# Fused sliding-window attention and cosine-gated MLP on one core: masks of four units written by ScalarE, x of eight units by DMA, and a new order of work

## The chip, the cores and the metric

The kernel runs on one core of a Trainium2 chip. The metric is the device time of one execution in microseconds (us); a comparison takes the median of several runs. The engines are named as in the profile: PE (TensorE, matmuls), DVE (VectorE), ACT (ScalarE), POOL (GpSimd) and SP (SyncE, which here only issues DMAs).

## The reference

Eight batches of eight heads, 576 tokens, 64 columns each. Attention has a window of 128 tokens and a bias that falls linearly with the distance; its output, as x (4608 tokens by 512), goes through an MLP with a cosine gate.

```python
scores = scale * np.matmul(q, k.transpose(0, 1, 3, 2))
bias = slopes[:, None, None] * (-np.abs(rel).astype(np.float32))[None, :, :]
mask = (rel >= 0) & (rel < window)
scores = np.where(mask, scores + bias[None], -1000000000.0)
attn = np.exp(scores - np.max(scores, axis=-1, keepdims=True))
attn = attn / (np.sum(attn, axis=-1, keepdims=True) + 1e-09)
x = np.matmul(attn, v)          # to (4608, 512)
h = x @ w_in                    # (512, 2048)
out = (h * np.cos(h)) @ w_out   # (2048, 512)
```

## The kernel before

**Attention** is cut into units. A batch has nine: four pairs of heads times G = 0 or 1 (the first and the second 256 tokens), and a tail of 64 tokens. A unit's score (L529 for a tail, L539) goes to two PSUM banks; ACT takes the exponential (`exps`, L590, L598); DVE multiplies by a mask table `emask` that holds window and bias together (`mask`, L611, L623; the table is built at the start, L460 and L465); PE multiplies by v (`pv`, L640 to L656); DVE divides (`norm`, L681 to L712). Two units share one score op, which waits as a whole for all that it reads. x is then transposed for the MLP, by PE with a copy on ACT or DVE (`x_pe`, L742 to L753) or by a DMA transpose on SP (`x_dma`, L762, L768). There is an older second way for the mask: `seed` (L554 to L579) has ACT write the scaled distances `dif` into the banks, the score adds to them, and the unit has no multiplication. The setting `SEEDN` says for how many pairs of units of a phase the first unit is seeded; it is empty here.

**q, k and v.** Batches 0 and 1 are transposed on PE (`qk_transposes`, L483, copies L500/L501). From batch 2 on, q and k are loaded as they lie (`load_nat`, L385, five DMAs each for `qnat` and `knat`) and transposed by two DMAs on SP (`dma_transposes`, L396 and L399, to `qt` and `kt`). v is loaded in five tiles (`load_v`, L375). All loads are issued by POOL, all DMA transposes and stores (L1095) by SP. Buffers are double, so batch b reuses those of batch b - 2.

**The MLP** runs over nine chunks of 512 tokens. The first product is L975 (chunk 0), L782, or L876 in a form with fewer products from chunk 6 on; ACT takes the cosine (L787, L940, L980) and DVE multiplies (L791, L943, L984). The second product is L1067 (L1161 for chunk 0), with sums made by DVE (L1003, L1031, L1046), a copy or sum (L1052, L1090) and the store.

**Order.** Attention of batch 0 comes first; then phase c (0 to 5) of attention, with 8, 10, 10, 12, 14 and 9 units, goes with chunk c. This program order only says what each op reads and writes. What runs when is said by a text at the head of the file, `TABLE`: `follow` decodes it into one list of all ops, and for copies that either ACT or DVE may do, into the engine. `emit` puts each engine's ops into its queue in this order, with waits on semaphores where another engine's op or a DMA must be done. Every queue is in order: an op that waits holds up everything behind it on its engine, and on POOL and SP this includes the DMAs behind it.

The settings that the change touches are read in `attention`:

```python
if g // 2 < SEEDN.get(phase, 0):
    two = sorted(two, key=lambda u: u[1] == "t")
    seed(two[0], 0)
...
first = (S * u[0] + (512 if u[1] == "t" else 256 * u[2])) // CH
after.append((first > phase + 1 or g < XD.get(phase, 0), u, ub, n))
```

Here `g` counts the units of a phase in steps of two, S is 576 and CH 512; a unit whose entry is true goes to `x_dma`.

Of the kernel before, what the change touches and what calls it, by code (L numbers as in the profile page):

```python
# [14 lines left out]
B, H, S, D = 8, 8, 576, 64  # L15
# [12 lines left out]


TABLE = (  # L30
    'c-nPV2Y6If7JmPfH!Wo*A%PHdEHqifjs=k}tV#(GFqBXPBn4$bu`FK_%_4*%1ObV(K#D*JSt&-E!h-'
    '0xDvPKfD@{Z`QYO7kX6D^JciMYzU|;fHUhcd1+;jf_Kj&N_3_w#jJy552L+3%Pc;zlP#H-yktj(-'
    'pEjqM{ck}PJwCrB3q-'
    '{9M;&d$5qHR9WADS}~;_2H1xbO#`q+wdtgon`B>6%HyG|f?3%VnDsdnr<5N0St5ZZ)?8zmXNGD<Zg2=y6N`U+Gy?'
    '$F$*GyJWJoN!r+3anTS_iMU&FrmJy)q1{k##U*rYHRJHq^Dy35b!Y@oPU}o$A?_9;n<O%5Xs0l2&{m^^1BgNm_9P'
    '~pqObs4C1TN&{Qy{6(86~%nA#%H5NW^O=4`d2vLnc~h(_}2&mQcz_^`@$G{b79x#rnLjt-93Hcj0-'
    'yv%|m2e+*e0cZK}!+72b)WUaJT8@pXD+fk0N6bOV1gB(Si4?NA5T2-'
    '!JB(zEKr!Mj%{>;HUNYjab!Z7$qCql;L3G!CjefR+FFk(bw73vr<2ntCbb8MB)_5dQYyf6J%<J=0tY;ul(MgN&rc'
    'O0s&EiG$uIcm#Y~Vab;v#yqnaVrE7GY>V-A}Btqa`;P_Nv&jvF#{*7WM`>VMkre&#)Wy?uO_aV#gax-'
    'm{4=v5trFP6j>R?Tw2c0rY#J*M(j<PaOY>o)>#w^hUa2)xJ2kX>J~-'  # L40
    '#3SczLYEI#)13`0UMgZCvSU&r@KXVhQx8AYHOt^~S#t385v1pL)39f1&X4(!RY_VSn%~;N7Le~0Vt5k)3C!7qncH'
    'Sb_KKyP6<WQBL=(H{om`}^2hwehkBNkN1f6-'
    '=6Jf`#n1*9F&|{#~8ip5b`?XFO3>mnmKg4fqM&X#D2BXTu`vb#MxEL-'
    '2=FZh<=U!>)?uhVjo~ev?pC0h90j^d!W2#$W>Vg}3Lez;yMB~`dF58D5!*GHZ4bkokcrZJo8XMBIs3+J`c0!*&!='
    'cNak2M(+9t6%k<c;_TI5&xT-;_~SjMe)zLQ?kr-'
    '9G)}so_oZgT~!nS)>B%(>F{i(nL<%Kma6dPT_kIY8xqVGm@6sSZY)QY;}3kyZHF!JjrNbPWohF6A1kpQae^Jz>4Y'
    'nMq|4ag_#Z%abX$X0Qx{bdg5-'
    'w!C^Sy0wzSSv6YO*7!5g5KOZPW>L)jeqDWi^PVfHiNt_&bV&I7<#pb?el1f*R3lvbBscPqQM6(|M=#E!7MQtWiEo'
    '^$q8jetWg{{laSk`ID;w6<lHL!It@CI3ZRWxET-dy=6bdfZi^BN)-'
    'kx6rkxYh^Af7Y$CX%W0qP@nf!;+_cuy#JAV$$(>L5)aS8M@n1a32RRL3Yb{W0a`!VJ8|o4{JEnxs(L});p(&v8a9'  # L50
    'u_yO{KZHL$YuW?tu(Sy-'
    '!vCGTmAdZpg4wXLtycpkG<<E5@OtDZg=!_1h1+Njmjw*z0aL)7QnhFOPv(elHPlI>oe%EXgvk}suL+RHI+l!oPEe'
    'ttc)y)KY7q-'
    'GO9HpEp~!82*s>_!_J5TR{@5f%EL7h^Wh(4l4fbO%j~jd783&`#My06C4>3;+Is6L%3tT|^hYe#$tr1&iB&6{dwW'
    'wmj!;Baz_4=p8Jja_9ps>tY{=<;GUvOwSAXGq+K`;>!KNrH|ImXY(ASTzHFN^apdvpSj*r6^VK)$8H@P=`NPcPO&'
    'XkYSBhFw`irt0gqb!LQPqlVQC7VwU?z)4yP6n<)+6xUk=rH29r)HJ=#nkkufV0J5o_@v9wsQWd0@&P$WT0e*0vOC'
    'WIl=#9la*x}LDtWaQG=0xl2(#f%Kz3QWi+K|tR$xwKh#_K~ywPUk>V_~X988-'
    'dL$7M*|kTUzrMQ~>ttJm@GYT>9QFLiQ#JGHIu^Q5UX9joXGsV+1N~s5tf4rg&Z0t843@yK)VUZ;eO{vvf>bj#_<{'
    'E{YJE13lG{)N}UY3D6Y>lsCkRX4ja{$9_e$IQETy;j`zD56VwIGwJ{vRRhIkkY72;<?OL;WxyDsbjLJ`d?#gik4L'
    '%OwvOj>3X-Yk5pe`ia}jeHouYwjx-lYe?zUO*6w~{=z!E<7?VOdoJcyIBk3;YN22T&Udsl*?z2EoT*eN`VQ(2lOw'  # L60
    '$ie!%Cd#CND}y^H-5G~apWoVM#%(x$>q1=4UeA7@v$>FHVpXpRNz-`z1w9-2S&rNI|0<^yIkuIxJ1&2qr-'
    'yn-P&*BAkwbEg<YgZWM`B<Ux7!?;yxT0hEB9Poq9_H<xB+6$<+&1*V*jXQ=!i##UhbBC-HxJ9b4f>O5FQM$GVlYY'
    '0;EzOMeT$+Oi@ir?~G>em;QF`Fb7Uw0-'
    ')DSUv5QX5E;wvHsQX@ok50m+CO*%wR0XM0gH$JNq(o?|pd}rcrfU%@Ny^NS$EwY}9WNlRrb}CwAb0!CyUIkX8zeE'
    't`lBMNi5`Z9289jS-byN0#8`Z0-K46!6u51NJvfI*I<pVOKD}#Bep<(EjKAJ>#OvyA?}aT-'
    'Eb<QtZWG>gAiq@nZu|-Z>5YIIxXgTPJ-Qv8(%8OF{x~utj?J<T~4~q=Mu!G!`B%o{U^X7EYfMjy|cFw5l`KlR}P!'
    'Ka8_mW<8uzKs|eA|5Ic*_e7cdlcU3q+K^v!GU5I4-4igxj^A<ASLge=;<iQSZL!w7=WR?W#-'
    'vXhCLeN@7x(>g+{qRDABl6lLS<Fw>!h`LQKaFe(HMu)ipAva=P&;AW;|7_8}?>Xa&1&CWqRI3oTyJm0VHkMj~b-'
    'KU~R;VLVn(IO$x|2XD-#Cwa~YvoxGM@0FUnOnlZXB(9|3jhMQu{ARUV7(DVnyPJ@o)_f&pP-'
    '0v1&I@q5tK0fHEZqW2B6vpePz;Nsr3p!)OwvLraMQ%IB0%b!Fk8kvD!^ICX(d5SU`>)JBl;A)3x!^A~*gA1H!Njk'  # L70
    '9bb31AJ#9jLnSFn5nJP8V+>6WI*{{9$K=-'
    'Ii4(}ekB>9rlTbz8;dAV@$vsGY#Mm*p3)v9cI)0mEeyn;9Sk1Ej+_{IEB=6m(OWM%qp|L4FkV=POcUwRSz4?%tjO'
    '!EE7%nJVFo1y$1xLEKDW3+%V*`a_(LEi!<eA{Ja22J?)4@RI|7PRIIN8a6UkTIrQNx^0MmIX}Gdse33v8*ibI3(}'
    'Q6!`hQq7VFL0TWDyL%1z)LEb|Fqa2QJsRyz<9M$)jGC(Gyq6mu#GUiIyWiMn}lrw_vC^2CnX65Kq(JOA5auqsW#('
    'az6gPr;3Fs3vS*iFTO!lleCE-fW~K`s@;f-'
    'DuL7*vWwMFvwo)YDYK%Ys!&lL=}a$qa_Dqe_$j$%4|P%7Sk&C^p7|E-05OoaEoQU{w(_HKhuIl)N)0L6E?If-ndQ'
    'f>bOkomPRMj6=zXYB;2Fs8S$=8>KAS9bxj%$jo92RQykW$_h$ynL-'
    ';1n|B~0C{NjJ5M;#~HD{_qDyS92ASr8Q=(}$hf?wlN8Dh7U35CEE3Rb4eZHcVrLB=YO&ys+EVM&F9-'
    '>_E|awkyN8>TE$>Y^ZLfm%hXRv?#4)t*Y5EYzr4%5w1xWK3uw7gWYn<tfyI;9|8HRZ>;#t145fwkp%W<gb}oO8Vt'
    ';%~TDI391Zd3iT@kVuEmcuME+!AOkCeh?Xh408{MGRAGcvK=>2_;SOCz;Xi5FXBMh@##BcNK~)Hu608vNLvl*BDH'  # L80
    'GHNRFy;B3gs%n{7pj$fl+x7VWHhmHY6$LK<1t&5`BViq8BRfR0)!TR`@J<FZkbrVSDq@w=+*W79u-'
    'AsdYv9Vyey(st|R(RU84Bg0wsI(4aO|@>6G)${!)5eW-e@5K<&=Z_fWO<s>k5KMFa_g&GrXJ7L|{Z-'
    'kIjkN?mA0G*W>_y'
)


# [166 lines left out]
def bass_alibi_sliding__then__act_gcu_kernel(  # L253
# [8 lines left out]
    with ExitStack() as ctx:  # L262
        def sb(name, shape, dt=BF16):
            return ctx.enter_context(nc.sbuf_tensor(name, shape, dt))

        R = Plan(nc, ctx)
# [5 lines left out]
        FAST, SPRI, GS = range(1, NCH), 3, 4  # L272
        FAST1, WPRI, KPRI, APRI, MPRI, GPRI, TPRI, LPRI = range(6, NCH), 4, 1, 2, 4, 4, 4, 5
        KENG, DPEN, CENG = ("act",), 0, ("act", "dve")
        JN, PRE2, SEEDN, XD, LORD = (5,), (), {}, {4: 6}, 0
        SDPRI, NH, LWPRI, G1, S4IN, SPLIT = 1, 2, 2, 1, True, True
        TRIPLES = [(2, 3, 4), (5, 6, 7)]
        WGS = 4
# [8 lines left out]
        xT = sb("xT", [128, NPAIR, XR], F16)  # L287
# [16 lines left out]
        P = [Pall[:, i, :, :] for i in range(NP)]  # L304
# [938 lines left out]
        for c in range(NCH):  # L1243
# [26 lines left out]
            n = QUOTA[c] if c < len(QUOTA) else 0  # L1270
# [54 lines left out]
```

## Time and profile before

| what | us |
|---|---|
| runs | 299.79, 300.42, 299.76 (median 299.79) |
| the profiled execution | 299.71 |
| its span, first to last instruction | 298.0 |
| PE busy | 287.9 (97%) |
| DVE busy | 262.1 (88%) |
| ACT busy | 222.1 (75%) |
| POOL busy (issue of loads included) | 95.2 (32%) |

Line numbers are those of the kernel before; after the change the same lines have a number higher by one, as the new table is a line longer. In a row of the timeline the columns are start, duration, engine, line, operation, output <- input, shape and count, and in brackets the idle time of the engine before it and what ended it. In a row of the groups they are busy time and mean nanoseconds of one, then the idle time before. In a row of the DMA issues the last number is the median time from issue to landing. Busy times by stage have a start and end, the length, and then busy time and instructions of each engine in turn.

### The profile page before, as it was taken

The numbers are of one execution on the slowest core, as the hardware profiler recorded it, in microseconds if no ns is written. First come the engines' busy times: TensorE is split into PE (matmuls) and PEld (weight loads), VectorE is DVE, ScalarE is ACT, GpSimd is POOL, SyncE is SP. The second block draws the span as 40 slices with busy tenths as digits, with TensorE's granted clock in tenths as the row PEclk, the third lists the DMA queues.
The fourth block names the chain that finished last, engine by engine and source line by source line (L and its number), as shares of the span: only waits on it lengthen the run. The fifth ranks groups of instructions, "written<-read, shape, count | busy, mean of one in ns | idle before, by whom it ended". The sixth has DMA issues, their size and how long they took to land.

```text
span 298.0 us, 7278 instructions
## 1 busy us (share of the span) xinstructions
PE 287.9 (97%) x2974; PEld 205.2 (69%) x2974; DVE 262.1 (88%) x522; ACT 222.1 (75%) x318; POOL 95.2 (32%) x122
## 2 busy tenths in 40 slices
PE   2899999999999999999999999999999999999996
PEld 2678845446874586458854788547768888888884
DVE  3879877599977999899999999999999999999972
ACT  5788878689757889688777878579778758778620
POOL 7997000599642303991195005000000000000000
PEclk9999999999999999999999999999999999999999
DMA  7999999999999994999999939973131400041033
GB/s 153 173 205 208 207 169 146 180 196 155 136 175 147 130 187 90 142 173 173 169 170 133 163 85 130 159 164 74 21 79 21 150 2 0 2 141 37 10 134 106
DMA packets 147729, 37.96 MB, mean 127 GB/s; under 512 B 133360, under 2 KB 146416, under 8 KB 147696
## 3 DMA queue, kind: packets, MB, share of 16 engines
q0 software_dynamic: 99344, 18.10, 79.7%
q1 hardware_dynamic: 48352, 19.41, 34.5%
q8 instruction: 23, 0.38, 0.5%
q14 instruction: 10, 0.08, 0.1%
HBM read 36.70 MB, written 9.44 MB: 155 GB/s over the span
## 4 chain that ended last, share of the span: by engine, by line
PE 94%; DVE 2%; POOL 1%; issue 1%; ACT 1%; POOLq 0%; DVEq 0%
PE ps L1067 33%; PE ps L782 24%; PE ps L876 11%; PE ps L539 5%; PE ps L975 5%; PE ps L1161 4%; PE ps L653 3%; PE ps L656 2%; PE ps L742 2%; PE ps L483 2%; PE ps L529 1%; DVE kt L501 1%; PE ps L640 1%; PE ps L642 1%; PE ps L1138 1%
## 5 line engine op out<-in xcount | busy, mean ns | idle before, releaser
L1067 PE MATMUL ps<-w_outb,gT 128*128 128x256 f16 x512 | 82.3, 273 | 0.0
L782 PE MATMUL ps<-xT,w_inb 128*128 128x512 f16 x336 | 82.2, 379 | 0.0
L787 ACT ACTIVATE cos<-ps,halfpi 128x512 f32<-128x512 f32 x84 | 54.9, 687 | 18.9 <-PE ps L782 13.9
L598 ACT ACTIVATE p<-ps 128x768 bf16<-128x768 f32 (+1 forms) x64 | 55.6, 915 | 11.5 <-PE ps L539 9.5
L791 DVE TENSOR_TENSOR gT<-ps,cos 128x512 f16<-128x512 f32 x84 | 54.5, 686 | 5.5 <-ACT cos L787 5.1
L1067 PEld LDWEIGHTS ps<-w_outb,gT 128*128 128x128 f16 x512 | 48.2, 98 | 12.5 <-issue 1.3
L782 PEld LDWEIGHTS ps<-xT,w_inb 128*128 128x128 f16 x336 | 31.7, 98 | 31.1 <-DVE gT L791 1.5
L375 POOL DMA_DIRECT2D vp<-in_v_dram x40 | 34.3, 892 | 53.1 <-PE ps L656 35.3
L1067 PE MATMUL ps<-wsum,gsum 128*128 128x256 f16 x256 | 38.5, 273 | 0.0
L623 DVE TENSOR_TENSOR p<-p,emask 128x768 bf16<-128x768 bf16 (+1 forms) x64 | 38.0, 615 | 0.3
L385 POOL DMA_DIRECT2D qnat<-in_q_dram x30 | 25.5, 918 | 23.9 <-DMA qt<-qnat 23.9
L1052 ACT ACTIVATE ob<-ps 128x512 f32<-128x512 f32 x33 | 19.6, 598 | 13.7 <-PE ps L1067 11.2
L385 POOL DMA_DIRECT2D knat<-in_k_dram x30 | 25.7, 948 | 9.3 <-DMA kt<-knat 7.0
L1067 PEld LDWEIGHTS ps<-wsum,gsum 128*128 128x128 f16 x256 | 23.2, 98 | 4.0 <-issue 0.5
L876 PE MATMUL ps<-xT,w_inb 128*128 128x256 f16 x132 | 24.8, 273 | 0.0
L696 DVE TENSOR_TENSOR xnats<-ps,rec 128x256 f16<-128x256 f32 x56 | 21.9, 420 | 0.5
L539 PE MATMUL ps<-qt,kt 64*128 64x128 bf16 (+1 forms) x320 | 20.1, 253 | 1.3 <-DVE kt L501 1.3
L653 PEld LDWEIGHTS ps<-vp,p 128*128 128x128 bf16 x256 | 16.0, 99 | 4.3 <-issue 1.0
L653 PE MATMUL ps<-vp,p 128*128 128x65 bf16 x256 | 18.9, 196 | 0.1
L1067 PE MATMUL ps<-wsum,gT 128*128 128x256 f16 x112 | 18.1, 273 | 0.0
L539 PEld LDWEIGHTS ps<-qt,kt 64*128 64x128 bf16 x320 | 11.9, 98 | 8.6 <-issue 3.6
L1161 PE MATMUL ps<-w_outb,gT 128*128 128x512 f16 x64 | 17.6, 380 | 0.0
(111 smaller groups left out, 478.0 us busy)
## 6 DMA issues: line engine op xcount, KB each, us to landing
out_dram<-ob SPq DMA_DIRECT2D x35, 256.0 KB, 2.7
vp<-in_v_dram POOLq DMA_DIRECT2D x32, 128.0 KB, 6.9
qnat<-in_q_dram POOLq DMA_DIRECT2D x24, 128.0 KB, 7.1
knat<-in_k_dram POOLq DMA_DIRECT2D x24, 128.0 KB, 10.8
w_inb<-in_moe_w_in_dram POOLq DMA_DIRECT2D x4, 512.0 KB, 10.5
w_outb<-in_moe_w_out_dram POOLq DMA_DIRECT2D x4, 512.0 KB, 21.8
gsum<-in_q_dram POOLq DMA_DIRECT2D x1, 576.0 KB, 15.5
gsum<-in_k_dram POOLq DMA_DIRECT2D x1, 576.0 KB, 17.6
```

Of the source, the lines that this page charges most:

```text
L375: op("pool", [lambda e, t=t, rows=rows: e.dma_start(vp[b % 2][0:rows, t, :, 0:64], v[b, :, 128 * t:128 * t + rows, :].rearrange("h p d -> ...
L385: fns.append(lambda e, t=t, rows=rows: e.dma_start(nat[which][b % 2][0:rows, t, :, :], src[b, :, 128 * t:128 * t + rows, :].rearrange("h p ...
L539: ins = e.matmul(ps[:, banks[x], c0:c1], keys_ap(b, x, pr, kc), query_ap(b, x, pr, qb, 128 * nb), start=c0 == 0 and (b, pr, G) not in seed ...
L598: op("act", lambda e: e.activation(P[i][:, :, 0:hi], src_[:, :, 0:hi], ACTF.Exp, scale=0.125), w=held + [("P", i)], occ=920 if G else 691, ...
L623: op("dve", lambda e: e.tensor_tensor(p, p, m, ALU.mult), r=[("EM", h0), ("EM", h1)] + ([] if G else [("EM2", h1)]), w=[("P", i)], occ=600 ...
L653: ins = e.matmul(o, P[i][:, x, d0:d0 + 128], V[:, kc, h, 0:65], start=True, stop=not two)
L782: op("pe", lambda e, kc=kc: e.matmul(ps[:, bank, :], w_in[:, kc, 128 * fc:128 * fc + 128], xT[:, kc, r0:r0 + CH], start=(kc == 0), stop=(k ...
L787: op("act", lambda e: e.activation(cosb[ci][:, :], ps[:, bank, :], ACTF.Sin, bias=halfpi[:, 0:1]), r=["halfpi"], w=[("B", bank), ("cos", c ...
L791: op("dve", lambda e: e.tensor_tensor(gT[gi][:, fc, :], ps[:, bank, :], cosb[ci][:, :], ALU.mult), r=[("cos", ci)], w=[("B", bank), ("g", ...
L876: op("pe", lambda e, i=i, kc=kc: e.matmul(ps[:, bank, 256 * i:256 * i + 256], left(kc, p0 + i), right(kc), start=(start and i == 0 and kc ...
L1067: op("pe", lambda e, t=t, p=p: e.matmul(ps[:, bank, 256 * t:256 * t + 256], left(p, slice(128 * t, 128 * t + 128)), right(p), start=(start ...
L1161: op("pe", lambda e, t=t, fc=fc, bank=bank: e.matmul(ps[:, bank, :], gT[gi][:, fc, 128 * t:128 * t + 128], w_out[:, fc, :], start=(fc == 0 ...
```

## The change

Two settings and the order. `SEEDN` becomes `{3: 2, 4: 2}`: the first unit of each of the first two pairs of phases 3 and 4 is seeded. In phase 3 these have G = 0 (two activations of 256 and two of 128 columns each), in phase 4 G = 1 (two of 512 columns each), twelve activations in all; their four multiplications at L623 go. `XD` becomes `{4: 6, 5: 2}`. The table is written anew for the list of ops that results.

```diff
 TABLE = (
-    'c-nPV2Y6If7JmPfH!Wo*A%PHdEHqifjs=k}tV#(GFqBXPBn4$bu`FK_%_4*%1ObV(K#D*JSt&-E!h-'
...
+    'c-nnd30PF+8b0qVXP9BwA-'
...
-        JN, PRE2, SEEDN, XD, LORD = (5,), (), {}, {4: 6}, 0
+        JN, PRE2, SEEDN, XD, LORD = (5,), (), {3: 2, 4: 2}, {4: 6, 5: 2}, 0
```

What the new table holds, decoded: the same 2974 matmuls in another order; three copies of q and k transposes and three copies of x more on ACT and fewer on DVE, and one copy at L1052 fewer on ACT and one more on DVE; 36 DMA transposes of x, as before. On POOL the load of v tile 3 of batch 6 stands ahead of the five loads of K of batch 6, where it stood behind them; on SP K's transposes of batch 6 stand behind seven transposes of x and one store after Q's, where they stood behind three transposes.

More of the change, by code (lines that the diff above doesn't have):

```diff
@@ L30 @@
 TABLE = (
-    'c-nPV2Y6If7JmPfH!Wo*A%PHdEHqifjs=k}tV#(GFqBXPBn4$bu`FK_%_4*%1ObV(K#D*JSt&-E!h-'
[L32 to L80, printed above, removed]
@@ L81 @@
-    'GHNRFy;B3gs%n{7pj$fl+x7VWHhmHY6$LK<1t&5`BViq8BRfR0)!TR`@J<FZkbrVSDq@w=+*W79u-'
-    'AsdYv9Vyey(st|R(RU84Bg0wsI(4aO|@>6G)${!)5eW-e@5K<&=Z_fWO<s>k5KMFa_g&GrXJ7L|{Z-'
-    'kIjkN?mA0G*W>_y'
+    'c-nnd30PF+8b0qVXP9BwA-'
+    '4>*)GWQJZJOO~H?=I(a4EegAf{rX;T1(KyNr4>Ma^)<Oi>FE(nQIn$GWy?i{@@O(=^lESY{YtU}j*>f4~3CFmuk}'
+    'a}Uf}{{4Hu_kI6gFdLd-H^bE|vSuLeR(p-nqer8uQPkCS#ntL?kErc{%66X0-'
+    '^{H21D>m$wO8UQI)C%`It{*h<{oJ3!x|*5WHzBTq8MloeqD<PG)x23qW@J*L~KQu)0!|%r}|hE;K1bvOh5OeR(0V'
+    'gsbhB_<cB^d9y7r8ljc#nhrpS+^pcha?G*ye<zBo?XhUejMQVAWHx6kAX{qz=c68Imeu~QHacFo|8zWycj7~(<8e'
@@ new lines @@
+    'nkSsyZSLwW87a+`$(QzIfDW<jsMaDA=Oqw;n&PoE>jNRE-Ojco?>}ZbLY$zZGpqg!RpLwO#6}cqCD9#^M@`<98zE'
+    'Q%9r8%*NVyc{oZn>;;6^(R(OR57!q%%M<A1%Rx*NQp#6Pi)RU-'
+    'c|V2+QNv2dpblXuk)RRb)<h1fJ&Yb_r4ZiK$h0i7FKFrm5)$l@`)7!2sP~l6vpCG=U}gIE=l*v16}}vOH3b)KyU|'
+    '$`_1N|t^k#=SOb+b^qTGhf$sCrt=4d!PKnzeF+gLs@w4poJrPLsDa`%g~J6dC`d2gaD1C?g*3_%|bSLW)hZb^7+8'
+    'Ma~ix(hw<i=4-'
+    '<{B{8k{)$}Kvo#Id@xevp1L;~Uo!_kIwNB$1w@1?~Mpy5ne4E)bZiCL_?za)?rni<*)?k{CnAtz~oV}9roqJoi9Q'
+    'O4Y5x}ff$Zj*?Na9LV4Be}h+9KrvSYuF)7%PQYgW1v+JF=wsJL@?tw92`JlYVvmymi2WnsxShG4CLgFfuuh9>XJN'
@@ new lines @@
+    '>Ae6w#HXC!nyu!)YT-'
+    '#dKcM{S6TcT^;E1~(!)c{uy0H4+=t+pt%EOz)N<;T^#5Z(=v%^iqLQfQ~g~5)Fm9Epna6N|VTzL2z(6PcD7vjQM#'
+    'EZsSamSQRW3gjI84~y4I#R`Hd2MVN#d<9M*Wyg~-'
+    'h+SPu$)34V5)oiqbGN;k$c!!8BU1c^v3pAO!<lBl8L#cP&UfcX!6!>n6`F&u{6C9NX~y9gi#IXzJ%gluq-'
+    '`lNwfn^QVbhYFblQ<QdcUcVcnLQt1~ySq4_mW+B6d)us)+EY6}{uIs|8!J8XdKM03CIa9V5{jV}h5nFmiEocwW=v'
+    'l+S(Z7PA)$Xs1`3|mn9>od3`uj2fudYEBzApShDUmvBjMc0CIJ)*G0D&;QC)H+coMu<z7Rfupn%+`)bJJa)|;Zg<'
+    'A4oyVuISXi%H8XRfZLq+y&_b9lCmieUp+K}V<vBvU0cWg#8=;!)^P2Zo&fmoQ`Y(GV@NMxs3!s6h$(@@@nv1lTq}'
@@ new lines @@
+    '#dhVBZPX$Q{}lw+=jC7L!ziU8Ci!avjpOjfL7sV<D{aeXF&wfBQoiy$P?&RgF7S2-uAwL`r8m*-'
+    'R;i5Nl`f`Dn(CtP!EiXp82qFr7cR<VNlhDX85EW4)-'
+    'Fj`sUTGqCCFXS9#}DB%;g*&#Z_a@*%y*Zq_5(|LN4a@xk7L{IS?qQoXb3ht62R0A}{If-'
+    'M{&_&W$a~$bWPkA_pUc@3j#~PD1!|`&_y*Ij{E;jMst1=9$fSImEOWwlUM88F}Qc?z8Vf7$PjmYpZXWFc#D+#d+5'
+    '6w-(gFXoV1Uh)%X06I%4O)qU&Z<Iebu8#k#TEF(l?*h*ZNV50uZ-;qkiQs0C)Dg^6YSABYv$M0+-'
+    'HEKoz4e3e)w6PgvVs4*P_~pIrXb%(Ys?MB46WDZ_JBHwiZf8w`82#$kXgJlJSx)qj3e#xsxamHPL9|buN&HtSWV5'
+    '{65E+Mhy!s)_Gh%<r;`2J>ES9^d2#z&$S1CwV*g@`{ajyxpUjz;m*b^^F0lvxpT!kBvnvIn)bJVyqS?$o~=jrhTS'
@@ new lines @@
+    '9eoJN(WpTM!+w3{_LkX2Lx1N6k{LW~DK0#eH<wJ9G(@rYiGs1Mtb+>E>|ph~|fZEKoCJUB3Mf7F2Q^jv;Jho{B%O'
+    '~M5IP~O@sQ<J;Vt~4^v@VapB=ym(h_tcr*ecObU0WSkPlD%Y$bC_2Xmfe3(gWPaKa#+1QL~Su^3UP@BAd!Xu@?Wp'
+    'n?Ses+mq(rFFP*;>^Ont9wvIsBlRE`J^ryc~AbM<m>g|{CL-xBEQ0d*zcx>orT9Iw2GR3j}sU+B%53`$a1cN(8+O'
+    'Kv7t`N}Be;zS~KhJWFHS4>Eo+&3wJUpa{K095Hzvg^;_S`G?FPryAm&@ehZS~s7IV<ce&$5vGA@ed$_vwA63#2^S'
+    'I~Q6OT9H=`in;Hp9GQ&UQ*-XW0(9nTF>n7q#@g*tw@F**W3ou&>$Xi;dvj6K?RlG)S;-'
+    'Tzc%kRDZ8?7+e$j+&)36@RZ{$<Nf40*-'
@@ new lines @@
+    'dZ`<Jnrr>=u@mNL%g4Z@^XwX1l1dxWOk4E(AmgY)A;!hLCnlk29JZ$xClxnme2`8=Sfi(%u6D`=Nk>P7{Q6GSuGs'
+    '1~*2IKfpFv3|jTllorWCL4`u<)Ww;aTXBMgPc^SwrT)v+CkC>v2aCUif2oVnQD^TrXPr^7r9<+ju!&}7Nj`*O4Xv'
+    'tcNh2<PQF&wraVnmoI4L^AO>>BkEw+AVwg^xs}Wg!qqLs}Bu-Vb4?webVMhJ}p*Kix1Ouxl?1T>)#xT*oT0h@x<|'
+    'pHjm>taBC30z{G-'
+    'qS$OHdivJ9prrCp6KjQirmv^w_v;U4fl8HR*Pe>6pp2<Z+tjXk8#Cgi(!VZxf^Nr*2aXL2AF(wm5T={LQ$cmA&_+'
+    'Nw<>PmFDiHC=mV-'
+    '&FSl}6&&WaMk{NKb8<13e$7eKTz<rjkmxrp;PaGWO^dba}R5{En0Zw>vv4#~#0Of9;UZZ;FUL_hi@TokX6mx@OUN'
@@ new lines @@
+    '?8`x44myU~L0><MLu4h~Ne^5@3ckXPi3Jm##kkKoa4XWOcpnn>Cve_5N%Z>@4ES`EcQYh%6r~XUDactw-'
+    '&?M{<0#>*X4-LbgT0_dbDvUOM)@d5SNyRg>(>#!EtN8MQQM8le#p-'
+    'yF232i4ZexIJ4*w&5&0}r>l?1|_!CALTecnUfppd&QHRR~bRrQ1fzhA982{%V@{hhOLXNjs@V3dx@wKBzj>X%_SH'
+    '*nY<ZnUnSICzXsA_4icw>UUjHVDQLd#;5eVA_+!QWN!VE*pDTKS!|bmo!dcsmQK0eqpTR?k=q7=phGvshZ{8B;{r'
+    '(#;nnq?S-5_*c)=Ed#^)-sDb9+1x(`Q-'
+    'm$wb1Z=Xm;wZKWXvC#e{TOsikmVC%2X)eRDm2Ii8?4bUb!<^U~0u+Em13T$W&vhXrO4%{LE73$vXn^FUKMTx(7yJ'
+    's=1hA*@6oEAi4yXsX-HznP)*zs*Cv2l(}JkWeKX3`O2A!kV-'
@@ new lines @@
+    '8D^r9S{39TcNizP}xU@6{ei8G8*4Y4yo0~O0uNl~$tsU*gHi4Inqe3t|zn-'
+    '~iw6bo9H8VrTtgDaRyvrLg>6&;z9s{tpI0+wO11UjmdDhO)zt8&>Y2{Ni2PDUbEaGf!gfC9n{ih~6iSAc*1xFw}%'
+    'lyNIX8)SlNTM0r@VbMy;2Qm*y5LA?FF;F?L-'
+    'bj7p$kwKm3}dRvS&N6VV6$fd7*!%rz$bT=OTkpG?`y&o>t`y2mA)6Cx5@~WcBf(+yBkHBDl@G(t6YatOe}b3QZ)<'
+    '!&lLKVe>pj-ga#Z;5ie61Bol(v!esfY<sr1PTQvr13kVjd!kvQc-'
+    '@6z{KH~5S{^~U#PGG8Hf^vLGRwGsTXJf)$;ZsOZk(eN*s6Ywq>`b}ku@(}yvT8xN%V|YvEvkTp;6nljn)!CTmb6G'
+    '}Z<o*-OhJ`Mw44|qiwyD?SWD+Xh?0M5xm*qiEZ70=wu=QFjZ`{pz1y}r8K`{Cp9b<#wLh{T*JDZp4n8ZeRu&j6U-'
@@ L84 @@
+    'i*KeU5DHYHH_aDp4@C|NWoQ*j@G`WtaZ}f4iH&'
 )
```

## The prediction

> **What bounds the kernel now.** I read the page first (busy time by engine, the clock, the chain of work that ended last), then a table of busy time by stage.
>
> ```profile
> span 298.0 us, 7278 instructions
> ...
> PE 287.9 (97%) x2974; PEld 205.2 (69%) x2974; DVE 262.1 (88%) x522; ACT 222.1 (75%) x318; POOL 95.2 (32%) x122
> ...
> PE 94%; DVE 2%; POOL 1%; issue 1%; ACT 1%; POOLq 0%; DVEq 0%
> ```
> ```profile
> core 0: us, PE busy (x) PEld busy (x) DVE busy (x) ACT busy (x) POOL busy (x), PEclk, DMA share, GB/s
> 5.70:20.00 14.30, 13.03 (x191) 10.27 (x191) 11.26 (x29) 12.37 (x21) 14.30 (x19) 1.00 1.49 187
> 20.00:132.00 112.00, 111.86 (x1121) 70.66 (x1119) 96.08 (x205) 88.42 (x135) 56.15 (x68) 1.00 1.70 164
> 132.00:165.00 33.00, 33.00 (x341) 21.59 (x340) 31.30 (x70) 25.93 (x37) 15.74 (x19) 1.00 2.04 160
> 165.00:295.00 130.00, 129.96 (x1327) 102.64 (x1325) 121.73 (x211) 92.16 (x123) 4.88 (x6) 1.00 0.45 80
> ```
>
> PE carries 94% of the chain that ended last. From 20 to 295 us it is idle for 0.14 + 0.00 + 0.04 = 0.18 us, at granted clock 1.00. So relief of DVE or ACT in the middle of the kernel has almost nothing to give. What is left to gain lies before 20 us, where PE idles 14.30 - 13.03 = 1.27 us after its first instruction. What can be lost is anything that makes PE stop, because PE's queue is in order and there is no idle time behind a stop to take it up: each microsecond lost stays lost.
>
> The two orders hold the same 2974 matmuls, so PE's own work is the same in both. The sum therefore starts from the profiled execution's 299.71 us (span 298.0 and 1.7 around it; the median of the runs is 299.79, 0.08 higher).
>
> **Part 1: masks by ScalarE in phases 3 and 4.** Two units with G=0 and two with G=1 lose their DVE multiplication at L623 and get distances written by ACT ahead of their scores.
>
> ```profile
> L623 DVE TENSOR_TENSOR p<-p,emask 128x1024 bf16<-128x1024 bf16 x32 | 21.1, 681 | 0.1
> L623 DVE TENSOR_TENSOR p<-p,emask 128x768 bf16<-128x768 bf16 x32 | 17.0, 550 | 0.2
> ```
> ```profile
> L460 ACT ACTIVATE emask<-dif 128x256 bf16<-128x256 f32 x8 | 2.8, 404 | 2.0 <-POOL dif L434 2.0
> ...
> L1052 ACT ACTIVATE ob<-ps 128x512 f32<-128x512 f32 x33 | 19.6, 598 | 13.7 <-PE ps L1067 11.2
> ```
>
> DVE loses 2 x 0.55 + 2 x 0.68 = 2.5 us. ACT gets four activations of 256 columns (0.40 each, L460), four of 128 columns (not in the trace; above zero and not more than the 0.40 of twice the columns, so I take 0.3) and four of 512 columns (0.60, L1052): 1.6 + 1.2 + 2.4 = 5.2 us. ACT is idle for 33.00 - 25.93 = 7.1 us from 132 to 165, and for 37.8 us in the 130 us after it, so the added work has room; without that cover its price is up to 5.2 us less DVE's 2.5. On ACT the seed waits for nothing new: its bank comes free with ACT's own exps of the unit before. The wait it adds is PE's: the score waits for the seed where it waited for those exps, and behind it stand the chunk matmuls. If ACT is behind there, PE stands. I cost it at nothing, between -0.2 (the whole steady idle) and +1.2 (the two seeds of one G=1 unit, 2 x 0.60, in full).
>
> **Part 2: x of eight units by DMA.** The setting names the first two units of phase 5 beside the first six of phase 4. In the code a unit also goes by DMA whenever its tokens begin more than one chunk ahead of the phase: phase 4 begins at token 5 x 576 + 256 = 3136 (chunk 6, above 5), phase 5 at 4032 (chunk 7, above 6). So these units go by DMA already, and 36 transposes of x stand in both orders. Nothing is moved; cost 0.
>
> **Part 3: the new order, at the start.** ACT also takes three more q/k copies and three more x copies from DVE and gives one output copy back. Most lie where PE is covered. Not so in the first 18 us:
>
> ```profile
> 9.04 1.51 ACT L598 ACTIVATE p<-ps 128x768 bf16<-128x768 f32 x2 [0.17 <-PE ps L539]
> 10.57 0.88 ACT L500 ACTIVATE qt<-ps 128x640 bf16<-128x640 bf16 x1
> 12.07 1.51 ACT L598 ACTIVATE p<-ps 128x768 bf16<-128x768 f32 x2 [0.62 <-PE ps L539]
> 14.21 2.85 ACT L598 ACTIVATE p<-ps 128x1024 bf16<-128x1024 f32 x3 [0.63 <-PE ps L539]
> ```
> ```profile
> 11.79 1.57 DVE L501 COPY kt<-ps 128x640 bf16<-128x640 bf16 x2
> ```
> ```profile
> 13.50 1.04 PE L539 MATMUL ps<-qt,kt 64*128 64x256 bf16 x12 [0.38 <-DVE kt L501]
> ```
> ```profile
> 17.96 0.94 PE L975 MATMUL ps<-xT,w_inb 128*128 128x256 f16 x7
> ```
>
> Before, the first G=1 score starts at 13.50, released by DVE's copy of kt; 0.71 later ACT has its exps at 14.21, and PE comes to the first chunk at 17.96, from where it does not stop. In the new order ACT has a mask (2.8/8 = 0.35) between the first two exps, and one of the two kt copies (0.88 by the q copy's row) behind the second pair of exps; that copy releases the G=1 score. PE now does the second pair of scores ahead of K's transposes, so the 0.62 wait goes. Along ACT: 9.04 + 0.76 + 0.35 + 0.76 + 0.88 + 1.51 + 0.88 = 14.18, plus the 0.14 from the end of DVE's kt copies (13.36) to PE's start: about 14.3, 0.8 late. ACT then also has four xT copies ahead of the chunk's matmuls, where it had three, but PE needs the fourth only some six matmuls later. I take **+0.7**, bounds 0 (the saved wait pays for the copy) and +0.9.
>
> **Part 4: the new order, K of batch 6.** Every load of q, k and v is issued by POOL and every transpose and store by SP, each in order. Two things move. On POOL, v tile 3 of batch 6 (it needs the buffer that the last tail product of batch 4, L640/L642, reads) now stands ahead of the five loads of K of batch 6. On SP, K's two transposes (L396, L399) now stand behind seven transposes of x instead of three.
>
> ```profile
> 129.10 4.31 POOL L385 DMA_DIRECT2D knat<-in_k_dram  x5
> 133.24 1.73 POOL L375 DMA_DIRECT2D vp<-in_v_dram  x2
> 147.62 0.89 POOL L375 DMA_DIRECT2D vp<-in_v_dram  x1 [12.65 <-PE ps L656]
> ```
> ```profile
> 148.79 0.19 PE L642 MATMUL ps<-vp,ptail 128*128 128x65 bf16 x1
> ```
> ```profile
> 145.41 4.03 SPq L396 DMA_TRANSPOSE qt<-qnat  x1
> 149.47 1.25 SPq L399 DMA_TRANSPOSE qt<-qnat  x1
> 150.77 5.61 SPq L768 DMA_TRANSPOSE xT<-xnats  x3
> 156.43 6.92 SPq L396 DMA_TRANSPOSE kt<-knat  x1
> 163.38 1.25 SPq L399 DMA_TRANSPOSE kt<-knat  x1
> 164.67 5.11 SPq L768 DMA_TRANSPOSE xT<-xnats  x4
> ```
> ```profile
> 172.57 0.41 PE L529 MATMUL ps<-qt,kt 64*128 64x64 bf16 x16
> ```
>
> Before, K is loaded from 129.10 on, ahead of POOL's 12.65 us wait for PE. After, it waits with v tile 3 for PE at 148.79 + 0.19 + 0.7 (part 3) = 149.7, and the five issues run, behind the v load's 0.89, from 150.5 to 154.8, the last issued at about 153.9. How long it takes to land depends on what else the DMA engines do:
>
> ```profile
> knat<-in_k_dram POOLq DMA_DIRECT2D x24, 128.0 KB, 10.8
> ```
> ```profile
> knat<-in_k_dram POOLq DMA_DIRECT2D x1, 64.0 KB, 14.4
> ```
> ```profile
> qnat<-in_q_dram POOLq DMA_DIRECT2D x3, 128.0 KB, 4.9
> ```
>
> These are the median of all K loads, K of batch 6 as it was at 133 us, and Q's loads issued from 145 to 151 us. So K is there at 158.8 (4.9), 164.7 (10.8) or 168.3 (14.4). SP comes to K's transposes at 150.72 + 0.7 plus seven transposes of x at 5.11/4 = 1.28 to 5.61/3 = 1.87 each: 160.4 to 164.5. The later of the two decides; I take 164.0, between SP's middle (162.4) and the median load (164.7), nearer the load. From the first issue to the landing of the second transpose, Q and K took:
>
> ```profile
> qt<-qnat SPq DMA_TRANSPOSE x2, 6.3
> ```
> ```profile
> qt<-qnat SPq DMA_TRANSPOSE x1, 7.5
> ```
> ```profile
> kt<-knat SPq DMA_TRANSPOSE x2, 9.9
> ```
> ```profile
> kt<-knat SPq DMA_TRANSPOSE x1, 12.8
> ```
>
> The pairs' medians (6.3 and 9.9) and the large ones alone (7.5 and 12.8) leave 5.1 for Q's small one and 7.0 for K's: 149.47 + 5.1 - 145.41 = 9.2 for Q, 163.38 + 7.0 - 156.43 = 14.0 for K. I take the middle, 11.6, as the queues ahead differ: K lands at 164.0 + 11.6 = 175.6. Its first user is the score of batch 5's tail and batch 6's first pair, one op that waits as a whole, at 172.57 on PE, with part 3 at 173.3. PE waits **2.3 us**; bounds 0 (160.4 + 9.2 = 169.6) and 9.0 (168.3 + 14.0 = 182.3). Before, K landed at 170.4, only 2.2 us ahead of its user, which is why so small a shift counts. The score stands in PE's queue ahead of L1067's matmuls, which can't pass it. On SP two stores and the next x stand behind K's transposes, which issue until about 172; the x is for matmuls after 180, so I add nothing for it.
>
> A rule speaks about the last link. The Trainium skill, page "DMA: Bandwidth & Descriptors", section "Latency and other measured facts", gives transposes by DMA an effective 261 GB/s. By it K's 576 x 512 x 2 B would be an estimated 2.3 us, landed near 167, and the total 300.4. The rows above (9.2 and 14.0) do not agree for transposes that share the engines with loads; the sum goes by the rows, and what the rule would bring is the first rival.
>
> **Sum:** 299.71 + 0 + 0 + 0.7 + 2.3 = **302.7 us**.
>
> **Rivals.**
>
> *K still lands in time.* If x's transposes go at 1.28, the loads land in under 6 us and K's transposes take Q's 9.2, K is there at about 170, before 173.3, and the startup loss alone remains: 299.71 + 0.7 = **300.4**. For it: Q's rows of the same stretch. Against it: three links must all be at their short end.
>
> *A longer wait.* The four loads of v behind K on POOL share the engines with it, as the loads at 129 us did. With 14.4 for the load (168.3) and 11.6 for the transposes, K lands at 179.9, a wait of 6.6: **307.0**; from 304.4 on I count it here. Against it: three of five transposes of x are then done, and the queue on SP is free.
>
> *Faster, by the start.* The one place with PE idle time is before 20 us: 1.27 us. If the two waits of ACT (0.62 and 0.63) go, as PE has the second scores early, and the moved kt copy is not the last thing that the G=1 score waits for, PE comes to the first chunk earlier. All 1.27 gives **298.4**; it decides for faster from 298.8 down, that is with L975's first matmul at 17.0 or before, and only if K also lands in time. Against it: the sum along ACT above, whose ops are all known.
>
> **How the numbers follow.** A measurement of this kernel tells 0.3% (0.9 us) from no change. The forecast (wait of 0.5 to 4 us, 300.9 to 304.4) gets 0.50: the middle of every link is in it. K in time gets 0.24: it ends 0.7 above before, inside 0.3%. The longer wait gets 0.18. Faster gets 0.08. So faster 0.08, same 0.24, slower 0.68. The range leaves out the faster case and most of the longer wait: 299.9 to 305.6, down to the K-in-time case with half a microsecond less loss at the start, and up to a wait of about 5.
>
> **What would show it.** Part 1: 60 multiplications at L623 instead of 64, new ACT rows at the seed's line, and no PE wait on ACT there. Part 3: the first G=1 score near 14.3 and L975 near 18.7. Part 4: POOL's K loads of batch 6 after 150 us instead of 129; K's transposes from about 164; and one PE gap of some 2 us at a score (L529 or L539) near 173, released by the DMA of kt. Without this gap, or with L975 at 17.96 or earlier, the prediction is wrong; a gap elsewhere of a microsecond or more would mean that I missed a queue.

## The result and the profile after

| | before | after |
|---|---|---|
| median (lowest to highest), us | 299.90 (299.76 to 300.42, 4 runs) | 304.62 (304.21 to 306.17, 4 runs) |
| ratio, 95% interval | | 1.0167 (1.0143 to 1.0190) |
| profiled execution, us | 299.71 | 305.01 |
| its span, us | 298.0 | 303.3 |

The changed kernel is slower by 4.7 us; the profiled executions differ by 5.3. Some executions have a mean granted clock of PE of 0.994 or less instead of 1.00 (one of the changed kernel's four, half of those of e3 and e10 below), and most of these are 0.5 us or more longer. The busy times by stage of the changed kernel, in the stages shown before:

```profile
5.70:20.00 14.30, 12.24 (x189) 8.67 (x189) 10.91 (x32) 13.29 (x24) 13.72 (x18) 1.00 1.47 182
20.00:132.00 112.00, 111.18 (x1106) 69.33 (x1107) 93.12 (x200) 88.93 (x137) 54.02 (x65) 1.00 1.74 165
132.00:165.00 33.00, 32.87 (x343) 21.70 (x342) 30.17 (x66) 28.10 (x47) 14.14 (x17) 1.00 1.41 131
165.00:295.00 130.00, 126.87 (x1294) 99.67 (x1292) 120.84 (x209) 93.53 (x125) 9.24 (x12) 1.00 0.59 84
```

PE's idle time is 2.06, 0.82, 0.13 and 3.13 us, against 1.27, 0.14, 0.00 and 0.04 before: 4.7 us more, with most of it after 165 us. The first stage doesn't compare as simply: the twelve matmuls of the first G=1 score took 1.04 us before and 0.62 here, and by 20.00 us PE had done 191 matmuls before and 189 here. What PE waited for, in the view of the waits of the changed kernel:

```profile
PE ps L654 <- issue: 2.5, 1, 2.5
PE ps L540 <- DVE kt L502: 0.9, 1, 0.9
PE ps L976 <- DMA w_inb<-in_moe_w_in_dram: 0.5, 1, 0.5
PE ps L540 <- ACT p L599: 0.5, 2, 0.3
PE ps L540 <- ACT kt L501: 0.4, 1, 0.4
PE ps L654 <- DVE p L624: 0.3, 1, 0.3
```

One stop of 2.5 us stands out, and it has no cause in this view: "issue" means that nothing which the profile shows ended it. The timeline has it here:

```profile
171.75 0.62 PE L540 MATMUL ps<-qt,kt 64*128 64x256 bf16 x12
174.89 0.19 PE L654 MATMUL ps<-vp,p 128*128 128x65 bf16 x1 [2.52 <-issue]
```
```profile
177.10 0.41 PE L530 MATMUL ps<-qt,kt 64*128 64x64 bf16 x16
```

It stands at a product with v, L654, and not at the score that first uses K of batch 6, which is the L530 at 177.10, a little later in PE's order. The queues of POOL and SP around it:

```profile
150.86 0.88 POOL L376 DMA_DIRECT2D vp<-in_v_dram  x1 [27.25 <-PE ps L643]
151.73 4.20 POOL L386 DMA_DIRECT2D knat<-in_k_dram  x5
155.86 2.50 POOL L376 DMA_DIRECT2D vp<-in_v_dram  x3
158.27 4.28 POOL L386 DMA_DIRECT2D qnat<-in_q_dram  x5
162.42 3.44 POOL L376 DMA_DIRECT2D vp<-in_v_dram  x4
```
```profile
161.23 6.44 SPq L397 DMA_TRANSPOSE kt<-knat  x1
167.71 1.29 SPq L400 DMA_TRANSPOSE kt<-knat  x1
```

POOL's wait is there, 27.25 us long, and K's loads behind it. But the last group of loads holds something that the prediction had not looked for: its second load, at 162.42 + 1.88/2 = 163.4, is v tile 3 of batch 5, one batch earlier, which the product at L654 needs. The account of the change above names K alone, but the table also moved v tiles 3 and 4 of batch 5 from ahead of K of batch 6 to behind it. The row of the first two loads of that group, their median time from issue to landing, and K's last transpose:

```profile
162.42 1.88 POOL L376 DMA_DIRECT2D vp<-in_v_dram  x2
```
```profile
vp<-in_v_dram POOLq DMA_DIRECT2D x2, 128.0 KB, 11.4
```
```profile
kt<-knat SPq DMA_TRANSPOSE x1, 7.0
```

163.4 + 11.4 = 174.8 is when v landed, and PE went on at 174.89; K landed at 167.71 + 7.0 = 174.7. The two can't be told apart by time alone: that is what the experiments are for. At the start PE and ACT read:

```profile
13.80 0.62 PE L540 MATMUL ps<-qt,kt 64*128 64x256 bf16 x12 [0.42 <-ACT kt L501]
...
17.58 0.97 PE L976 MATMUL ps<-xT,w_inb 128*128 128x256 f16 x6
...
20.48 0.61 PE L976 MATMUL ps<-xT,w_inb 128*128 128x256 f16 x4 [0.54 <-DMA w_inb<-in_moe_w_in_dram]
```

The first chunk begins at 17.58, 0.38 earlier than before (with the faster matmuls named above), and then PE waits 0.54 for w_in.

### The profile page after: what moved, and what is told of

It is laid out like the page before. It is cut to its first block, busy times and chain, and to the rows that moved or that the text cites. A ratio compares the mean times of both kernels' runs of the same rounds, so it can differ in the third digit from the quotient of the medians.

```text
span 303.3 us, 7297 instructions
## 1 busy us (share of the span) xinstructions
PE 288.7 (95%) x2974; PEld 203.9 (67%) x2974; DVE 258.2 (85%) x513; ACT 227.3 (75%) x335; POOL 95.0 (31%) x122
## 4 chain that ended last, share of the span: by engine, by line
PE 78%; DMA 10%; POOL 3%; ACT 3%; DVE 2%; issue 2%; DVEq 0%; ACTq 0%
PE ps L1068 31%; PE ps L783 21%; PE ps L877 11%; DMA w_outb<-in_moe_w_out_dram 8%; PE ps L540 4%; PE ps L1162 3%; PE ps L654 2%; ACT cos L788 2%; PE ps L657 1%; POOL vp L376 1%; DMA ob<-in_q_dram 1%; PE ps L743 1%; DVE gT L792 1%; PE ps L641 1%; POOL w_inb L408 1%
## 5 line engine op out<-in xcount | busy, mean ns | idle before, releaser
L783 PE MATMUL ps<-xT,w_inb 128*128 128x512 f16 x336 | 81.9, 379 | 0.0
L1068 PE MATMUL ps<-w_outb,gT 128*128 128x256 f16 x512 | 81.0, 273 | 0.1
L788 ACT ACTIVATE cos<-ps,halfpi 128x512 f32<-128x512 f32 x84 | 53.7, 687 | 17.1 <-PE ps L783 11.2
L792 DVE TENSOR_TENSOR gT<-ps,cos 128x512 f16<-128x512 f32 x84 | 54.1, 684 | 7.7 <-ACT cos L788 7.3
L783 PEld LDWEIGHTS ps<-xT,w_inb 128*128 128x128 f16 x336 | 31.6, 98 | 32.3 <-DVE gT L792 2.0
L1068 PE MATMUL ps<-wsum,gsum 128*128 128x256 f16 x256 | 40.4, 273 | 0.0
L624 DVE TENSOR_TENSOR p<-p,emask 128x768 bf16<-128x768 bf16 (+1 forms) x60 | 35.4, 612 | 2.0 <-ACT p L599 1.8
L877 PE MATMUL ps<-xT,w_inb 128*128 128x256 f16 x132 | 23.7, 273 | 0.0
L654 PE MATMUL ps<-vp,p 128*128 128x65 bf16 x256 | 18.6, 195 | 3.0 <-issue 2.5
L540 PE MATMUL ps<-qt,kt 64*128 64x128 bf16 (+1 forms) x320 | 19.4, 245 | 1.9 <-DVE kt L502 0.9
L654 PEld LDWEIGHTS ps<-vp,p 128*128 128x128 bf16 x256 | 15.8, 98 | 7.7 <-issue 4.5
L1068 PE MATMUL ps<-wsum,gT 128*128 128x256 f16 x112 | 19.2, 273 | 0.0
```

The source lines that it names most:

```text
L540: ins = e.matmul(ps[:, banks[x], c0:c1], keys_ap(b, x, pr, kc), query_ap(b, x, pr, qb, 128 * nb), start=c0 == 0 and (b, pr, G) not in seed ...
L624: op("dve", lambda e: e.tensor_tensor(p, p, m, ALU.mult), r=[("EM", h0), ("EM", h1)] + ([] if G else [("EM2", h1)]), w=[("P", i)], occ=600 ...
L654: ins = e.matmul(o, P[i][:, x, d0:d0 + 128], V[:, kc, h, 0:65], start=True, stop=not two)
L783: op("pe", lambda e, kc=kc: e.matmul(ps[:, bank, :], w_in[:, kc, 128 * fc:128 * fc + 128], xT[:, kc, r0:r0 + CH], start=(kc == 0), stop=(k ...
L788: op("act", lambda e: e.activation(cosb[ci][:, :], ps[:, bank, :], ACTF.Sin, bias=halfpi[:, 0:1]), r=["halfpi"], w=[("B", bank), ("cos", c ...
L792: op("dve", lambda e: e.tensor_tensor(gT[gi][:, fc, :], ps[:, bank, :], cosb[ci][:, :], ALU.mult), r=[("cos", ci)], w=[("B", bank), ("g", ...
```

## The experiments

**Theory V:** the stop waits for v tile 3 of batch 5, which stands in POOL's queue behind a load that waits for PE. **Theory K**, the prediction's: it waits for K of batch 6. **Theory F:** it is no wait for data (a fetch of instructions). Moves are shown as a queue's order; all other queues stay. The rows of e6 to e8 have the line numbers of the kernel before.

**e1, v tile 3 of batch 5 first.**

```diff
 POOL
+v tile 3 of batch 5
 v tile 3 of batch 6 (waits for PE)
 K of batch 6; v tile 0 of batch 6; v tiles 2, 4 of batch 5; Q of batch 7; v tile 2 of batch 6
-v tile 3 of batch 5
```

> The changed kernel with one move in POOL's queue: the load of v tile 3 of batch 5 goes ahead of the load of v tile 3 of batch 6, which waits for PE until 148.9 us; K of batch 6 stays behind that wait. Theory V (PE's 2.5 us stop at 172 us, which the trace gives no cause for, waits for v tile 3 of batch 5, eighth in line behind the blocked load): the stop at L654 goes, and K, which landed at 174.7, is next at the score; that is due at 174.6 without the stop, so 0 to 0.8 us of wait remain and the time is 302.1 to 302.9. Theory K (as in the prediction, the stop belongs to K of batch 6) and theory F (it is a late fetch of instructions): the stop stays at 2.5 us, 304.6.

Measured: 302.19 us (301.26 to 302.74), ratio 1.0071 (1.0052 to 1.0091). The stop at L654 is gone: V holds, K and F fall. K was not waited for either: its last transpose went out at 165.94 and landed 6.8 later at 172.7 (the pair's median is 9.3, the large one's 11.8), and the score started at 173.66. But a new stop appears, again without a name:

```profile
PE ps L783 <- issue: 1.2, 1, 1.2
```

**e2, v tile 3 of batch 6 last.**

```diff
 POOL
-v tile 3 of batch 6 (waits for PE)
 K of batch 6; v tile 0 of batch 6; v tiles 2, 4 of batch 5; Q of batch 7; v tile 2 of batch 6
 v tile 3 of batch 5
+v tile 3 of batch 6
```

> The changed kernel with v tile 3 of batch 6 moved behind v tile 3 of batch 5 in POOL's queue, so that K of batch 6, two tiles of v of batch 5 and Q of batch 7 are no longer behind its wait. Theories V and K: no stop at 172 to 177, 304.6 - 2.5 = 302.1, and K lands before 165. Theory F: stop stays, 304.6. What is left over the kernel before (about 2.2 us) is then the start and waits of a few tenths elsewhere.

Measured: 302.51 (302.19 to 303.41), ratio 1.0095 (1.0077 to 1.0113). No stop from 165 to 190 us. Whichever way the blocked load is taken out of the way, 2.1 to 2.4 us come back. One thing came otherwise than expected: K doesn't land before 165. Its loads go out at 123.60, but its transposes only at 161.09, as late as in the changed kernel (161.23), because SP comes to them no earlier:

```profile
161.09 5.98 SPq L397 DMA_TRANSPOSE kt<-knat  x1
```

**e3, the memsets at the start.**

```diff
 DVE
+memsets of v's buffer and the tail's buffer
 cast of q
-memsets of v's buffer and the tail's buffer
```

> The changed kernel with DVE's two memsets of v's and the tail's buffers put back ahead of the cast of q at the start. Theory W (the loss at the start is the wait for w_in's second quarter at 20 us, whose load POOL issues 0.73 us later because the v load ahead of it waits 0.91 for DVE's memset): that wait of 0.54 and its like at 25 us shrink, 304.0. Theory A (the loss is ACT's longer chain to the first G=1 score, as predicted): no change, 304.6.

Measured: 304.54 (303.53 to 305.93), ratio 1.0158 (1.0132 to 1.0184): no difference that can be told. POOL's v load starts at 5.37 where it waited until 6.28 for DVE (the changed kernel's row, then this one's):

```profile
6.28 1.76 POOL L376 DMA_DIRECT2D vp<-in_v_dram  x2 [0.91 <-DVE vp L444]
```
```profile
5.37 1.76 POOL L376 DMA_DIRECT2D vp<-in_v_dram  x2
```

PE's wait for w_in is no longer among its waits, as W expects. But W isn't shown: e4 keeps POOL's old order, issues that part of w_in at 9.87, and waits 1.1 us for it; e5, with the move of this run and the issue at 9.65, waits 0.3. From issue to landing the load took 9.5 (e9) to 10.3 us (e5), and that decides as well.

```profile
PE ps L976 <- DMA w_inb<-in_moe_w_in_dram: 1.1, 1, 1.1
```
```profile
PE ps L976 <- DMA w_inb<-in_moe_w_in_dram: 0.3, 1, 0.3
```

The stop at L654 stayed at 2.4 us, and a wait of 0.3 for another load of v came at 43 us. The three executions with a granted clock of 0.999 or more took 303.53 to 304.10, those of the changed kernel 304.21 to 305.01: some 0.6 less, as W has it, but on three executions each.

**e4, the seeds alone.** The kernel before with `SEEDN` of the changed one, each seed on ACT right behind the op that frees its bank, all else in the old order.

```diff
-SEEDN {}
+SEEDN {3: 2, 4: 2}
```

> The kernel before, its order untouched, with the seeds of phases 3 and 4 alone: four multiplications on DVE go, twelve activations come, each right behind the op that frees its bank. Theory N (ACT has the room, PE is the bound): 299.9, within 0.5 either way. Theory S (a seed holds up its score): each of four scores waits up to 0.6, up to 302; a wait on L575 shows in the trace. If DVE's relief counts: 299.0 or less.

Measured: 307.07 (306.95 to 307.18), ratio 1.0237 (1.0224 to 1.0250). Neither N nor the size in S: 7.2 us for four multiplications fewer, of which the wait of 1.1 for w_in (under e3) is no part of the seeds' cost. Its waits:

```profile
PE ps L540 <- ACT ps L575: 3.7, 2, 2.1
PE ps L540 <- ACT p L599: 2.5, 3, 1.3
```
```profile
132.85 0.70 ACT L575 ACTIVATE ps<-dif 128x256 f32<-128x256 f32 x2 [0.76 <-DVE gT L792]
...
134.91 0.70 ACT L575 ACTIVATE ps<-dif 128x256 f32<-128x256 f32 x2 [0.76 <-DVE gT L792]
```

The first score of a phase uses banks that the MLP's product on DVE (L792) frees. Before, DVE hands such a bank to PE; with a seed it goes from DVE to ACT to PE, and ACT, which waits, holds back the cosines and exps behind. PE's stops at the second pairs (1.31 and 0.95 us) are waits for these exps.

**e5, both moves (e2 and e3).** The diffs are those two.

> The changed kernel with the moves of both earlier kernels: v tile 3 of batch 6 behind v tile 3 of batch 5, and DVE's two memsets ahead of the cast. If the two losses add up (the stop of 2.5 us at 172, and about 0.5 at the start): 304.6 - 2.5 - 0.5 = 301.6. If the start's gain is given back by later waits for loads, as it was when it was made alone: 302.1 to 302.5. What stays over the kernel before belongs to the order on PE, ACT and DVE and the seeds.

Measured: 302.47 (302.31 to 303.12), ratio 1.0079 (1.0061 to 1.0097). No better than e2 alone; the unnamed stop of e1 is back:

```profile
PE ps L783 <- issue: 0.9, 1, 0.9
```

PE goes on at 187.20. The transpose of an x tail, issued at 179.40, landed 7.7 us later, at 187.1; in e2 it landed at 178.94 + 5.2 = 184.1, before PE needed it. Why it took longer here is open.

**e6, the late loads on the kernel before.**

```diff
 POOL, ten loads of the kernel before
-v tiles 3, 4 of batch 5
 v tile 2 of batch 4; Q of batch 6; v tile 3 of batch 4
-K of batch 6
 v tile 4 of batch 4; v tile 0 of batch 5
-v tile 1 of batch 6; Q of batch 7; v tiles 2, 3 of batch 6; v tile 2 of batch 5; v tile 0 of batch 6
+v tile 3 of batch 6 (waits for PE)
+K of batch 6; v tile 0 of batch 6; v tiles 2, 4 of batch 5; Q of batch 7; v tile 2 of batch 6
+v tiles 3 of batch 5, 1 and 4 of batch 6
 K and two v tiles of batch 7
-v tile 4 of batch 6
```

> The kernel before with ten loads of POOL's queue in the changed kernel's order: v tile 3 of batch 6 first, which waits for PE at about 148, behind it K of batch 6, v tiles 2, 4 and 3 of batch 5, Q of batch 7. Nothing else is moved. Theory V: PE stops for v tile 3 of batch 5 at about 171, 2 to 3 us, 302 to 303; SP's order is the old one, so K's transposes wait for K's loads too. If the stop needs the new order on the other engines: 299.9.

Measured: 302.46 (301.58 to 306.05), ratio 1.0107 (1.0055 to 1.0158). POOL's order alone costs 2.7 us by the medians, over half of the change's loss, on an otherwise untouched kernel; the interval allows 1.6 to 4.7. Not as one stop, though:

```profile
PE ps L1067 <- ACT ob L1052: 1.0, 1, 1.0
PE ps L653 <- issue: 0.8, 1, 0.8
```

The second stands at the product that needs v tile 3 of batch 5 again; the first is an output buffer whose store stands on SP behind K's late transposes, which no theory had named. Neither was tried by a move of its own.

**e7, the new order without the seeds.** `SEEDN` back to empty, with the four masks on DVE beside their neighbours, in the changed kernel's order.

> The changed kernel's order without the seeds: the twelve activations go, the four multiplications on DVE come back beside those of the units that share their scores. Theory N (part 1 costs and gains nothing in this order): 304.6 within 0.4. Theory S (the seeds cost): the 0.3 at 134 us (wait on L575 and the change of rows) goes, 304.2. If DVE's relief was a gain that other losses hid: 305 to 306.

Measured: 304.87 (304.35 to 306.08), ratio 1.0158 (1.0137 to 1.0179): no difference, N holds. In this run the profile does name what ended the stop:

```profile
PE ps L653 <- DMA vp<-in_v_dram: 2.3, 1, 2.3
```

**e8, the new order of the first 18 us on the kernel before**, for PE, ACT and DVE, with e3's move; POOL and SP as before.

> The kernel before with the changed kernel's order of PE, ACT and DVE up to the last attention op of batch 0 (some 18 us), the memsets ahead of the cast, and POOL and SP as before. In the trace of the changed kernel PE was 0.25 us ahead at 18 us, before the wait for w_in. If POOL's old order brings w_in in time: 299.6 to 299.8, a gain too small to tell. If w_in's landing bounds this place in any order: PE waits what it gained, 299.9 to 300.4. If ACT's chain is the loss at the start, as predicted: 300.6.

Measured: 300.16 (299.83 to 301.45), ratio 1.0007 (0.9995 to 1.0020). ACT's longer chain alone costs nothing that can be told.

**e9, three moves.** e5, and on SP:

```diff
 SP
+x tail of batch 4
 K's two transposes of batch 6
 stores and other transposes of x
-x tail of batch 4
```

> The kernel with both moves, and one more: on SP the transpose of batch 5's x tail goes ahead of K's transposes of batch 6, where it stood seven places behind them. If the stop of 0.9 us at L783 (186 us), for which the trace names nothing, is a wait for this transpose: the stop goes and the time is 301.6. If it is another DMA or no DMA: 302.5. The rest over the kernel before, some 1.5 us, is then waits of tenths.

Measured: 301.29 (301.26 to 301.45), ratio 1.0040 (1.0025 to 1.0055). The expectation calls the x tail batch 5's; it is batch 4's (its tokens from 576 x 4 + 512 = 2816 on belong to chunk 5, whose product stops). It goes out at 160.05 instead of 179.40 (e5's row, then e9's), and the stop at L783 is gone from the waits: a DMA it was.

```profile
179.40 1.25 SPq L763 DMA_TRANSPOSE xT<-xtail  x1
```
```profile
160.05 1.84 SPq L763 DMA_TRANSPOSE xT<-xtail  x1
```

**e10, the seeds alone, late.** e4 with each seed just ahead of its score.

> The kernel before with the seeds alone, as in the run that took 307.07, but each seed placed on ACT just ahead of its own score and not right behind the op that frees its bank. Theory H (a seed whose bank DVE's product frees holds up the cosines and exps behind it on ACT): ACT no longer waits early, and what is left is the handing over from DVE to ACT to PE at the first pair of each phase, 0.5 to 1.2 us twice: 300.9 to 302.3. Theory S (seeds cost wherever they stand): 305 or more. Theory N (free): 299.9.

Measured: 305.75 (304.45 to 306.92), ratio 1.0186 (1.0157 to 1.0214). H is too cheap. The place helps by 1.3 us of 7.2 by the medians, and by 2.2 at a granted clock of 1.00 (304.76, the middle of three, against the one of 306.95). The longest of the three stops, 1.96 us at 140.43, is at the second pair of phase 3, whose bank ACT's own exps free: there ACT comes to the seed late.

```profile
PE ps L540 <- ACT ps L575: 4.7, 3, 2.0
```

## Why the prediction was right in sign and short in size

The forecast was 302.7; the time is 304.62, above the forecast's own 304.4, in the part that the prediction gave to the longer wait (0.18), and inside the stated range. By the prediction's own signs its account of the start is wrong (L976 starts before 17.96) and it missed a queue (the stop is at a product, not at a score). By its steps:

- **The bound.** Right: PE is in order and full, and a stop stays to the end: taking away the one of 2.5 us returned 2.4 (e1) and 2.1 (e2). So is the sign that follows.
- **Part 1, seeds at nothing.** The number holds in the new order (e7), the reason does not. "The seed waits for nothing new" is true of a bank that ACT's own exps free; the first pair of a phase takes it from DVE's product. At a second pair ACT itself can be late, as the term's upper bound allows. In the old order the run with the seeds is 5.6 to 7.2 us longer (e10, e4; 1.1 of e4's is w_in). In the new order ACT waits for DVE 0.2 us at the seeds, where it waited 3.0 in e4, and PE has one wait of 0.13 us at L575.
- **Part 2, no effect.** Right as far as it was seen: 29 and 7 transposes of x in both profiles; not tried alone.
- **Part 3, +0.7 by ACT's chain.** The wrong step. The G=1 score came at 13.80, not 14.3, and L976 at 17.58, not 18.7; e8 shows that the chain costs nothing that can be told. What the trace has at the start is the 0.54 for w_in: POOL's v load waits 0.91 for a memset that the new order has behind a cast, and w_in's second part goes out at 10.51 instead of 9.78 (rows below, before and after). That the order causes this wait, and what the start costs in all, is not shown (e3).

```profile
9.78 2.28 POOL L407 DMA_DIRECT2D w_inb<-in_moe_w_in_dram  x3
```
```profile
10.51 2.28 POOL L408 DMA_DIRECT2D w_inb<-in_moe_w_in_dram  x3
```

- **Part 4, +2.3 for K.** The mechanism (a load that waits for PE at the head of POOL's queue) was right, the victim was wrong, and that the size agrees (2.5 against 2.3) is luck, as v's wait adds up from other links. The step that failed is the list of what stands behind the wait: it named K and missed v tiles 2, 4 and 3 of batch 5. K's own landing was close (predicted 175.6, landed 174.7), by two misses that offset each other: SP came to the transposes at 161.23, not 164.0, and they took 13.5 us, not 11.6. POOL's wait made SP stand only 1.5 us ahead of them (159.68 to 161.23), and with the early loads of e2 they still began at 161.09. Without v's stop its score would have come at 177.10 - 2.52 = 174.6: 0.1 of wait.
- **The missing term.** Waits of tenths were taken as zero. After e9's three moves 1.1 us stay over the 300.16 that the kernel before took beside it. By e9's busy times, below, PE idles 0.27 us from 20 to 132, 0.13 from 132 to 165 and 0.60 from 165 to 295: 1.00 where it was 0.18. What in the new order causes each was not tried.

```profile
20.00:132.00 112.00, 111.73 (x1112) 69.65 (x1110) 93.70 (x202) 89.62 (x138) 57.61 (x69) 1.00 1.81 169
132.00:165.00 33.00, 32.87 (x342) 21.59 (x341) 30.35 (x66) 28.09 (x47) 10.82 (x13) 1.00 1.64 148
165.00:295.00 130.00, 129.40 (x1320) 102.33 (x1319) 120.53 (x208) 92.89 (x124) 8.38 (x10) 1.00 0.47 77
```

Of the 4.7 us, e9 returns 3.3 by the medians (3.8 by the ratios, 1.27% of 299.9) by moving three DMAs or what they wait for, without touching a matmul. The Trainium skill's rate for transposes ("DMA: Bandwidth & Descriptors", section "Latency and other measured facts") would have had K landed in an estimated 2.3 us; from 161.23 to 174.7 it took 13.5 here, beside loads. No kernel tried beats the one before.

## What to carry to other kernels

When a load that waits for another engine moves forward in an in-order queue, list everything behind it, batch by batch, with the first user of each, and take the earliest; a familiar victim hides the others. A stop hides the next: behind the one for v stood, in e1 and e5, one of 0.9 to 1.2 us for x. A gain made ahead of a wait for a DMA can be lost in it; e5 beside e2 suggests this, and no run shows it alone. And an operation moved to an engine with idle time is free only if the hand-over that it adds is, and if that engine comes to it in time.

## What the runs showed of the hardware

A wait for a DMA can stand in the profile as "issue", with no releaser: in the changed kernel, and in e1 and e5, as the moves of e1 and e9 showed; for the changed kernel's wait e7 has the DMA's name. At such a stop the queue of the DMAs tells more than the view of the waits.

PE's first matmuls run at different speeds from execution to execution, though the granted clock of that stage reads 1.00: twelve of them took 1.04 us in the kernel before and in e3, and 0.62 in the changed kernel, which has e3's order on PE. What decides this is open.
